# Agent attention with experts on one core: sums as a column, blocks in the last batch, first queries behind the keys

## The chip, the cores and the metric

The kernel runs on one core of a Trainium2 chip. The metric is the device time of one execution in microseconds; the median of the runs is compared.

## What is computed

Agent attention for B = 4 batches of N = 11456 tokens with D = 128 channels and 49 agents, then a mixture of 8 experts (128 to 1024 to 128) in which each token goes to one expert.

```
def sm(a, b):
    s = scale * (a @ b.transpose(0, 2, 1))
    s = s - s.max(-1, keepdims=True)
    e = np.exp(s)
    return e / (e.sum(-1, keepdims=True) + 1e-09)
a2k = sm(agents, k)
agent_v = a2k @ v
q2a = sm(q, agents)
x = q2a @ agent_v
...
expert_idx = np.argmax(x @ w_gate, axis=1)
...
h = np.maximum(xe @ w1[e], 0.0)
out[mask] = gate_w[mask, None] * (h @ w2[e])
```

`gate_w` is the softmax of the logits at the chosen expert. Inputs and output are float32.

## The kernel before

**Tiling.** A batch's tokens lie in 12 chunks, eleven of 1024 (a tile of 128 partitions with 8 tokens each) and one of 192. Keys, values and queries are loaded by SP, a chunk at a time, into one ring of 13 buffers, `ld`. A chunk of keys or queries is scaled by powers of two and split into a high and a low float16 part (ACT makes the high one, L470, DVE the low one, L475; the scalings are POOL's, L462 and L464), turned by a transposing transfer, and multiplied with the agents on PE.

**Keys and values.** DVE keeps a running maximum of the key scores (`mx`, L563); `keymax` (L568 to L582) reduces it over everything. Then for each chunk: subtraction on DVE (L590), exponential on ACT (L595), an addition of the exponentials into `es` (L602, L605: on DVE in batch 0, on POOL later), and value products on PE (`values`, L618: eight pairs of float32 products of 128 columns a chunk). `agentvalues` reduces `es`, sums it over partitions with a product by ones, and divides. `choose` then takes the expert that most tokens of the batch are likely to want; its weights are split in the same manner, and the agents' values are multiplied into its first layer (`Ah` and `Al`, L881).

**Queries.** Scores (L531 to L533), maximum and exponential (L722, L723, L728), high and low half of the weights (`ehigh`, L738; `elow`, L746), a transposing transfer into `M`.

**Dense experts.** The chosen expert is applied to all tokens of the batch, in 23 groups of up to 512 tokens by 8 slices of the hidden layer: 184 steps a batch. A step is layer 1 (two products of 512 columns, L1465 and L1466), the high half of its result on ACT (`upper`, L1472), the low half on DVE (`lower`, L1477), and five steps later layer 2 (12 products of 128 columns, L1490) into a PSUM buffer `py` of the ring `Y`, which has two. At a group's end `store` (L1499) multiplies by the factors and `put` (L1507) sends 256 KB to the output.

**Leftovers.** Tokens that chose another expert are ranked (`ranks`), gathered by POOL (L332) into blocks of 128 tokens of one expert, and computed again: for a block, two loads of weights of 512 KB (`weights_ahead`), two splits (`weights_split`: ACT L1318, DVE L1321, the latter 1.28 us), layer 1 in two halves of 12 products (L1330 to L1332), its halves on ACT (L1337) and DVE (L1341), layer 2 (L1351 to L1353) into a `pyb` of the same ring `Y`, a scaled copy (`block_store`, L1358), and a scatter by POOL (`block_out`, L1368). Twelve blocks come from the first three batches and the first part of the fourth's table, two from the last batch.

**What sets the order.** Every piece is an entry of a `Plan`: a rank in steps of the dense experts, an engine, a cost, what it needs, and which buffers it takes and frees. `Plan.order` runs a simulated clock and lets each engine, when free, take the ready piece of lowest rank; the pieces are then written into each engine's queue in that order, and an engine executes its queue in order. Pieces of DVE other than those of the steps get DX = 8 added to the rank. SP's queue holds all loads, transposes and puts together. Before, blocks' products need the last layer 1 and layer 2 of the last batch (`("L1", z0 - 1)`, `("L2", z0 - 1)`), so they stand behind all of it; the weights of the first seven blocks are fetched and some split during the last batch.

Of the kernel before, what the change touches and what calls it, by code (L numbers as in the profile page):

```python
# [31 lines left out]
SPLIT0 = (True, False)  # L32
NQ = 2
M1E, M2E, M2L, ESE = 'D', 'DP', 'D', ['D', 'P']
# [8 lines left out]
DX, AX_, WSP = 8, 0, 1  # L43

LAG = 5

LT, LTS = 140, 6
# [134 lines left out]
def agent_moe_kernel(ctx, tc, q, k, v, agents, wg, w1, w2, out):  # L182
# [174 lines left out]
    def pick(x, c):  # L357
# [6 lines left out]
                mm0=1, mm1=1, cum=1, acc=1, es=1, mx=1, m1=1, lmax=1, W=2, ag=1, pd=2, ss=4, sck=6, scq=6, fr=2)  # L364
    plan = Plan(caps, ("S", "ld", "hl", "hTk", "hTq", "M", "mm0", "mm1", "Y", "sck", "scq", "cum"))
# [1335 lines left out]
```

## Time and profile before

| | |
|---|---|
| median of 2 runs | 1139.47 us (1138.49 to 1140.44) |
| the profiled execution | 1148.7 us, span 1146.9 us |
| busy over the span | PE 1036.3 us (90%), DVE 992.8 (87%), ACT 759.0 (66%), POOL 186.1 (16%) |
| front, to the first layer 1 | 0 to 83 us |
| four batches | from 83, 331, 574 and 817 us |
| tail with the blocks | about 1075 to 1146.9 us |

All times inside the kernel are microseconds from the span's start. A busy PE is counted by modelled ends of its matmuls. The granted clock is TensorE's, as a share of full speed; a stage below 1.00 had stretches at the lower of its two levels. Chains of waits follow the work that ended last back in time; a wait names who was waited for.

### The profile page before, as it was taken

How to read it: one execution, taken by the hardware profiler on the slowest of the kernel's cores; microseconds unless marked ns; L12 is line 12 of the kernel's file. 1: busy time of each engine (PE TensorE's matmuls, PEld its weight loads, DVE VectorE, ACT ScalarE, POOL GpSimd, SP SyncE). 2: the span in 40 equal slices, each digit the busy share in tenths (PEclk: the TensorE clock that was granted, in tenths of full speed). 3: DMA queues.
4: the chain of work that ended last, by engine and by line, in shares of the span. 5: the costliest groups of instructions: out<-in, count | busy, mean ns of one | idle time of the engine just before them, and what ended most of it. 6: DMA issues, size and time to landing. Idle time of an engine off the chain costs nothing.

```text
span 1146.9 us, 34925 instructions
## 1 busy us (share of the span) xinstructions
PE 1036.3 (90%) x14260; PEld 824.1 (72%) x14260; DVE 992.8 (87%) x2213; ACT 759.0 (66%) x1350; POOL 186.1 (16%) x367
## 2 busy tenths in 40 slices
PE   7659999999989999999989999999998788999774
PEld 7537777877767778777767777777776657777774
DVE  4778999997999999969999999878998797899774
ACT  6447878666678786765877886656665456575462
POOL 1000102033101110323011010331001311100132
PEclk8779999999999999999999999999999899999887
DMA  8438979793678969763778988726564545342440
GB/s 338 132 123 185 220 197 210 179 267 103 202 167 189 233 164 201 227 208 99 203 179 192 197 188 222 208 85 164 128 117 126 118 95 135 105 148 91 144 160 11
DMA packets 265668, 190.97 MB, mean 167 GB/s; under 512 B 217513, under 2 KB 230306, under 8 KB 265504
## 3 DMA queue, kind: packets, MB, share of 16 engines
q1 hardware_dynamic: 263648, 185.39, 63.6%
q0 software_dynamic: 1568, 2.25, 0.9%
q8 instruction: 113, 1.85, 0.7%
q10 hardware_dynamic: 288, 1.05, 0.2%
q14 instruction: 51, 0.42, 0.1%
HBM read 99.75 MB, written 36.43 MB: 119 GB/s over the span
## 4 chain that ended last, share of the span: by engine, by line
PE 53%; DVE 19%; DMA 16%; issue 8%; ACT 3%; POOL 1%; SPq 0%; POOLq 0%; ACTq 0%; DVEq 0%
PE py L1490 25%; PE ph L1465 8%; PE ph L1466 8%; DMA hT<-hl 7%; DVE hh L1477 7%; DMA M<-mm 4%; PE ps_small L618 3%; DMA ld<-in_q_dram 2%; ACT hh L1472 1%; PE ps_small L531 1%; PE ps_acc L618 1%; DMA ld<-in_k_dram 1%; DVE wsp L1321 1%; DVE hl L475 1%; PE ps_small L533 1%
## 5 line engine op out<-in xcount | busy, mean ns | idle before, releaser
L1490 PEld LDWEIGHTS <-hh 128*128 128x128 f16 x8640 | 536.1, 99 | 146.8 <-issue 14.8
L1490 PE MATMUL py<-w2h,hh 128*128 128x128 f16 (+1 forms) x5760 | 595.5, 220 | 4.4 <-DVE yo L1499 1.9
L1472 ACT ACTIVATE hh<-ph 128x512 f16<-128x512 f32 (+1 forms) x736 | 412.8, 583 | 243.9 <-PE ph L1466 213.2
L1490 PE MATMUL py<-w2l,hh 128*128 128x128 f16 (+1 forms) x2880 | 520.4, 220 | 0.7 <-issue 0.7
L1477 DVE SCALAR_TENSOR_TENSOR hh<-ph,hh 128x512 f16<-128x512 f32 (+1 forms) x736 | 472.0, 668 | 50.3 <-ACT hh L1472 47.6
L1465 PE MATMUL ph<-M,Ah 128*128 128x512 f16 (+1 forms) x736 | 277.0, 377 | 30.0 <-DVE hh L1477 26.5
L1466 PE MATMUL ph<-M,Al 128*128 128x512 f16 (+1 forms) x736 | 277.2, 377 | 1.7 <-DVE Al L881 1.7
L462 POOL TENSOR_SCALAR mul<-hb 128x1 int32<-128x1 int32 (+1 forms) x90 | 27.7, 308 | 494.5 <-DVE hb L455 477.4
L475 DVE SCALAR_TENSOR_TENSOR hl<-ld,mul,hl 128x1024 f16<-128x1024 f32 (+1 forms) x84 | 102.8, 1232 | 4.7 <-ACT hl L470 4.1
L1466 PEld LDWEIGHTS <-Al 128*128 128x128 f16 x736 | 72.2, 98 | 45.8 <-issue 38.5
L436 ACT ACTIVATE jk<-ld 128x1024 f16<-128x1024 f32 (+1 forms) x90 | 90.5, 1006 | 18.6 <-DMA ld<-in_q_dram 9.3
L470 ACT ACTIVATE hl<-ld,mul 128x1024 f16<-128x1024 f32 (+1 forms) x84 | 91.0, 1093 | 12.8 <-POOL mul L462 10.8
L1465 PEld LDWEIGHTS <-Ah 128*128 128x128 f16 x736 | 72.9, 99 | 14.5 <-issue 4.0
L531 PE MATMUL ps_small<-agh,hT 128*128 128x49 f16 (+1 forms) x630 | 58.5, 186 | 13.0 <-DMA hT<-hl 12.6
L531 PEld LDWEIGHTS <-hT 128*128 128x128 f16 (+1 forms) x630 | 51.6, 98 | 22.6 <-DMA hT<-hl 19.9
L1499 DVE TENSOR_TENSOR yo<-py,cs 128x512 f32<-128x512 f32 (+1 forms) x92 | 61.6, 669 | 2.0 <-PE py L1490 2.0
L533 PE MATMUL ps_small<-agh,hT 128*128 128x49 f16 (+1 forms) x630 | 58.1, 185 | 0.0
L532 PE MATMUL ps_small<-agl,hT 128*128 128x49 f16 (+1 forms) x630 | 58.1, 185 | 0.0
L532 PEld LDWEIGHTS <-hT 128*128 128x128 f16 (+1 forms) x630 | 50.9, 98 | 2.5 <-issue 0.6
L533 PEld LDWEIGHTS <-hT 128*128 128x128 f16 (+1 forms) x630 | 50.6, 97 | 0.0
L605 POOL TENSOR_TENSOR es<-es,S 128x392 f32<-128x392 f32 (+1 forms) x33 | 35.0, 1060 | 61.7 <-ACT S L595 61.0
L728 ACT ACTIVATE E<-E,ln,div 128x392 f32<-128x392 f32 (+1 forms) x48 | 33.0, 687 | 16.6 <-DVE E L723 15.8
(293 smaller groups left out, 1262.8 us busy)
## 6 DMA issues: line engine op xcount, KB each, us to landing
ld<-in_k_dram SPq DMA_DIRECT2D x44, 512.0 KB
ld<-in_q_dram SPq DMA_DIRECT2D x44, 512.0 KB
ld<-in_v_dram SPq DMA_DIRECT2D x44, 512.0 KB
out_dram<-yo SPq DMA_DIRECT2D x88, 256.0 KB
w1e<-in_moe_w_dram SPq DMA_DIRECT2D x17, 512.0 KB
w2e<-in_moe_w_dram SPq DMA_DIRECT2D x17, 512.0 KB
exps<-E SPq DMA_DIRECT2D x44, 196.0 KB
wn<-in_moe_w_dram SPq DMA_DIRECT2D x16, 512.0 KB
```

The lines of the kernel that those rows point to most:

```text
L436: nc.scalar.activation(jk[:p, :t * D], x[:p, :t, :].rearrange("p t d -> p (t d)"), AF.Square, accum_out=ss[:p])
L470: nc.scalar.activation(hl[:p, 0, :t, :], loaded[b, src, c][:p, :t, :], AF.Copy, scale=SC[src, c][0][:p, :1])
L475: nc.vector.scalar_tensor_tensor(hl[:p, 1, :t, :], loaded[b, src, c][:p, :t, :], SC[src, c][0][:p, :1], hl[:p, 0, :t, :], op0=ALU.mult, op ...
L531: nc.tensor.matmul(o, x[:, 0, i, :p], AG["h"], start=True, stop=False)
L532: nc.tensor.matmul(o, x[:, 0, i, :p], AG["l"], start=False, stop=False)
L533: nc.tensor.matmul(o, x[:, 1, i, :p], AG["h"], start=False, stop=True)
L1465: nc.tensor.matmul(ph[:, :nn], st['Ah'][:, f, :], m, start=True, stop=False)
L1466: nc.tensor.matmul(ph[:, :nn], st['Al'][:, f, :], m, start=False, stop=True)
L1472: nc.scalar.activation(hh[:, 0, :nn], ph[:, :nn], AF.Relu)
L1477: nc.vector.scalar_tensor_tensor(hh[:, 1, :nn], ph[:, :nn], 0.0, hh[:, 0, :nn], op0=ALU.max, op1=ALU.subtract)
L1490: mm_ = lambda l, r, **k: nc.tensor.matmul(o, l, r, skip_group_check=True, **k)
L1499: nc.vector.tensor_tensor(yo[:p, :n, :], py[:p, :n * D].rearrange("p (i d) -> p i d", d=D), cs.unsqueeze(2).broadcast_to([p, n, D]), op=AL ...
```

## The change

1. **Sums as a column.** A tile of values gets a 129th column of ones (`column`, written by POOL once the load has landed), the value products have 129 columns, and so has the accumulator. The sum of the exponentials is then the accumulator's last column; it is spread over the partitions by one product. `kexp3` with `es`, and the reduction in `agentvalues(0)`, are gone. A load of values writes 512-byte runs at a pitch of 516 bytes.
2. **First queries.** All key loads come before the first query's; the first two query chunks get ranks behind the keys.
3. **Blocks.** The products of the twelve early blocks get ranks within the last batch, from step 86 on, one in eight steps; weights are loaded 22 steps ahead of them and split 10 steps ahead, into buffers of `hTk` and `ld`. The last two stay behind the batch. The last batch's ranks and table come earlier and closer together.
4. **Engines.** In batches 0 to 2 every third store of a group goes from DVE to ACT, as four operations of 128 columns; in the last batch all. There `elow` goes from DVE to POOL.
5. **Costs and landing times** of the plan are changed, and the ring `Y` no longer serves its users in the order of their ranks.

```diff
-SPLIT0 = (True, False)
+K0 = 'UWUWUWUWUWUW'
+KO = (0, 1, 2, 3, 4, 5, 6, 7, 8, 9, 10, 11)
+KLO = (0, 1, 2, 3, 4, 5, 6, 7, 8, 9, 10, 11)
 NQ = 2
-M1E, M2E, M2L, ESE = 'D', 'DP', 'D', ['D', 'P']
+M1E, M1L, M2E, M2L, SE, SEL = 'D', 'D', 'DP', 'P', 'DDA', 'A'
+K0D, Q0, QF = 0, (-332, -296), -3
...
+LANDH, LANDM, LANDL = 2.0, 2.4, 2.4
...
-LT, LTS = 140, 6
+LT, LTS, LT3, LTS3 = 140, 6, 112, 1.5
...
-FE, FG, FGI = 24, 30, 28
-FL, FW, FWJ, WA, FS, SPA = 155, 92, 10.5, 7, 14, 7
-BL = 2
+FE, FG, FGI, FGS = 24, 30, 28, 2
+FL, FLI = 124, 1
+BB, BS, BLAG, BZ, WL, WS = 86, 8, 3, 3, 22, 10
+SLOT = ('hTk', 'ld')
...
-            x = loaded[b, src, c] = ldp.tile([P, 8, D], F32, tag="ld", name="ld")
-            nc.sync.dma_start(x[:p, :t, :], chunk_view({"k": k, "v": v, "q": q}[src][b], c))
...
+            x = loaded[b, src, c] = ldp.tile([P, 8, D + (src == "v")], F32, tag="ld", name="ld")
+            nc.sync.dma_start(x[:p, :t, :D], chunk_view({"k": k, "v": v, "q": q}[src][b], c))
...
+        def column(c):
+            _, p, t = chunks[c]
+            nc.gpsimd.memset(loaded[b, "v", c][:p, :t, D:], 1.0)
...
-        def kexp3(c):
-            _, p, t = chunks[c]
-            sc = S[c][:p, :t, :]
...
-            else:
-                es = AV["es"]
-                (nc.vector if pick(ESE[b > 0], c) == "D" else nc.gpsimd).tensor_tensor(
-                    es[:p, :t, :], es[:p, :t, :], sc, op=ALU.add)
...
-                nc.tensor.matmul(ps[r:r + w, :D], sc[:p, i * A:i * A + w], x[:p, i, :],
+                nc.tensor.matmul(ps[r:r + w, :D + 1], sc[:p, i * A:i * A + w], x[:p, i, :],
...
-                nc.vector.tensor_copy(acc, ps[:64 + A, :D])
+                nc.vector.tensor_copy(acc, ps[:64 + A, :D + 1])
...
-            if i == 0:
-                e1 = one.tile([P, A], F32, tag="e1", name="e1")
-                nc.vector.tensor_reduce(e1, AV["es"].rearrange("p t a -> p a t"), axis=AX.X, op=ALU.add)
...
-                nc.tensor.matmul(AV["pe"][:, :A], ones, AV["e1"], start=True, stop=True)
+                nc.tensor.matmul(AV["pe"][:, :A], AV["acc"][:64 + A, D:].broadcast_to([64 + A, P]), both[:64 + A], start=True, stop=True)
...
-                t, u = -390 + 4 * c, chunks[c][2] / 8
-                add(n_("load", "k", c), t - 4, "SP", 0.4, load, "k", c, take=[("ld", n_("k", c))], land=2.2, move=1.3)
+                t, u = -390 + 4 * KO.index(c), chunks[c][2] / 8
+                add(n_("load", "k", c), -395 + KLO.index(c), "SP", 0.4, load, "k", c, take=[("ld", n_("k", c))], land=2.2, move=1.3)
...
+            add(n_("column", c), base + t - 1, "POOL", 0.15, column, c, r=[n_("load", "v", c)])
...
+                t = Q0[c]
             else:
...
-                    t = max(t, -7 + c)
+                    t = max(t, QF + c)
...
-            tag = slots[(2 * u + j) % len(slots)]
+            tag = SLOT[j]
...
-            nc.vector.tensor_tensor(yo[:p, :n, :], py[:p, :n * D].rearrange("p (i d) -> p i d", d=D),
-                                    cs.unsqueeze(2).broadcast_to([p, n, D]), op=ALU.mult)
+            if pick(SEL if b + 1 == B else SE, g) == "D":
+                nc.vector.tensor_tensor(yo[:p, :n, :], py[:p, :n * D].rearrange("p (i d) -> p i d", d=D),
+                                        cs.unsqueeze(2).broadcast_to([p, n, D]), op=ALU.mult)
+            else:
+                for i in range(n):
+                    nc.scalar.activation(yo[:p, i, :], py[:p, i * D:(i + 1) * D], AF.Copy, scale=cs[:, i:i + 1])
...
-            add((b, "store", g), i + LAG + 0.7, "DVE", 0.6 * u, store, g, r=[("L2", i), (b, "factors", cl)], free=[("Y", (b, g))], take=[("yo", (b, g))])
+            se = pick(SEL if b + 1 == B else SE, g)
+            add((b, "store", g), i + LAG + 0.7, "DVE" if se == "D" else "ACT", 0.6 * u if se == "D" else 0.27 * n, store, g, r=[("L2", i), (b, "factors", cl)], free=[("Y", (b, g))], take=[("yo", (b, g))])
...
-        t = b * steps + LT
+        t, ts = b * steps + (LT3 if b + 1 == B else LT), LTS3 if b + 1 == B else LTS
         for i, (g, w) in enumerate(((x, 2.6), (x, 2.9), (x, 4.4), ("PE", 0.55), ("DVE", 1.1), ("SP", 0.5), ("DVE", 0.6), ("DVE", 0.6), ("DVE", 0.5))):
-            add(("ranks", b, i), t + LTS * i, g, w, next, gen, None,
...
-        t = l0 + FG + FGI * k_ if early else l0 + FL + 3
+        t = l0 + FG + FGI * k_ if early else l0 + FL + 5 * FLI
...
-            add(p + (i, "e"), t + 2 * i, g, w, go, r=r, **kw)
...
-        t = l0 + FW + FWJ * u if u < WA else l0 + steps + 3 * u - 40
-        add(("wa", u), t, "SP", 3.0, weights_ahead, u, r=[e] + ([("wa", u - 1)] if u else []), take=[("ld", ("wb", u, 0)), ("ld", ("wb", u, 1))], land=2.2, move=2.6,
-            head=("L1", l0 + min(int(FW + FWJ * u - 4), steps - 20)))
...
+            add(p + (i, "e"), t + (FGS if early else FLI) * i, g, w, go, r=r, **kw)
...
     for u in range(NS):
...
+        late = u >= NSE
+        t = z0 + 1 + BZ * (u - NSE) if late else l0 + BB + BS * u
+        y = "1" if late else "0"
+        add(("wa", u), t - WL, "SP", 2.0, weights_ahead, u, r=["table" + y] + ([("wa", u - 1)] if u else []), take=[("ld", ("wb", u, 0)), ("ld", ("wb", u, 1))],
+            land=2.4, move=2.6, head=("L1", int(min(t - WL - 6, z0 - 20))))
...
+            x, tag = (u, j), SLOT[j]
+            add(("wu",) + x, t - WS + 2 * j, "ACT", 1.05, weights_split, u, j, True, r=[("wa", u), "bscales" + y], take=[(tag, ("wsp",) + x)])
+            add(("wl",) + x, t - WS + 2 * j + 1, "DVE", 1.2, weights_split, u, j, False, r=[("wu",) + x], free=[("ld", ("wb", u, j))])
...
-            x, t = (u, hf), z0 + 2.4 * u + 1.2 * hf
-            add(("b1",) + x, t, "PE", 0.68, block_layer1, u, hf, r=[("g", g0, 18, "e"), ("wl", u, 0), ("L1", z0 - 1)] + ([("b1", u, 0)] if hf else [("b1", u - 1, 1)] if u else []),
...
+            add(("b1",) + x, t + 1.2 * hf, "PE", 0.68, block_layer1, u, hf, r=[("g", g0, 18, "e"), ("wl", u, 0)] + ([("b1", u, 0)] if hf else [("b1", u - 1, 1)] if u else []),
+                take=[("H", ("b",) + x)], free=[(SLOT[0], ("wsp", u, 0))])
...
+            add(("b2",) + x, t + BLAG + 1.2 * hf, "PE", 0.68, block_layer2, u, hf, r=[("bd", u, 0), ("bd", u, 1), ("wl", u, 1)] + ([("b2", u, 0)] if hf else [("b2", u - 1, 1)] if u else []),
...
+        add(("bs", u), t + BLAG + 2, "DVE", 0.3, block_store, u, r=[("b2", u, 1)], free=[("Y", ("b", u))])
+        add(("bo", u), t + BLAG + 6, "POOL", 1.2, block_out, u, r=[("bs", u)] + ([(B - 1, "put", g) for g in range(NG)] if late else []), land=1.5, move=0.2)
```

The first place is DVE's queue at the front, where the key scores' last part is (`S` and `mx` of 96x98 are the last key chunk's, `mq`, `E` and `mm` belong to the first query chunk, `m` to the reduction over the keys). Before:

```order
L722 TENSOR_REDUCE mq<-ps_small 128x8
L723 TENSOR_TENSOR E<-ps_small,mq 128x392
L551 COPY S<-ps_y 96x98
L563 TENSOR_TENSOR mx<-mx,S 96x98
L738 CAST mm_143<-E 128x8x49
L746 TENSOR_TENSOR mm_143<-E,mm_143 128x8x49
L568 TENSOR_REDUCE m_769<-mx 128x49
L574 TENSOR_REDUCE m_775<-ps_small 49x1
L576 TENSOR_SCALAR dg<-ident,m_775 49x49
L582 COPY mxb<-ps_small 128x49
L590 TENSOR_TENSOR S<-S,mxb 128x392 x6
```

After:

```order
L560 COPY S<-ps_y 96x98
L572 TENSOR_TENSOR mx<-mx,S 96x98
L577 TENSOR_REDUCE m_736<-mx 128x49
L464 TENSOR_SCALAR hb<-ss 128x1
L583 TENSOR_REDUCE m_747<-ps_small 49x1
L585 TENSOR_SCALAR dg<-ident,m_747 49x49
L591 COPY mxb<-ps_small 128x49
L599 TENSOR_TENSOR S<-S,mxb 128x392 x2
L484 SCALAR_TENSOR_TENSOR hl<-ld,mul,hl 128x1024
L599 TENSOR_TENSOR S<-S,mxb 128x392 x9
L599 TENSOR_TENSOR S<-S,mxb 96x98
L716 TENSOR_REDUCE mq<-ps_small 128x8
```

The last key's copy and maximum and the reduction now stand ahead of the first query's low part (`hl`), maximum and weights; they have one scaling of the query (`hb`) between them.

The second place is DVE's queue where blocks are computed (`wsp` are split weights, `hh<-ph` with L1341 before and L1338 after is a block's low half, with L1477 before and L1474 after that of a dense step, `yb` a block's scaled copy). Before, behind the last batch:

```order
L1358 TENSOR_SCALAR yb<-pyb,fgt 128x128 x3
L1321 SCALAR_TENSOR_TENSOR wsp<-w2e,tsm_17172,wsp 128x1024
L1321 SCALAR_TENSOR_TENSOR wsp<-w1e,tsm_17157,wsp 128x1024
L1321 SCALAR_TENSOR_TENSOR wsp<-w2e,tsm_17172,wsp 128x1024
L1321 SCALAR_TENSOR_TENSOR wsp<-w1e,tsm_17157,wsp 128x1024
L1321 SCALAR_TENSOR_TENSOR wsp<-w2e,tsm_17172,wsp 128x1024
L1321 SCALAR_TENSOR_TENSOR wsp<-w1e,tsm_17157,wsp 128x1024
L1321 SCALAR_TENSOR_TENSOR wsp<-w2e,tsm_17172,wsp 128x1024
L1321 SCALAR_TENSOR_TENSOR wsp<-w1e,tsm_17157,wsp 128x1024
L1341 SCALAR_TENSOR_TENSOR hh<-ph,hh 128x512
L1321 SCALAR_TENSOR_TENSOR wsp<-w2e,tsm_17172,wsp 128x1024
L1341 SCALAR_TENSOR_TENSOR hh<-ph,hh 128x512 x5
```

After, within the last batch:

```order
L1474 SCALAR_TENSOR_TENSOR hh<-ph,hh 128x512
L1318 SCALAR_TENSOR_TENSOR wsp<-w1e,tsm_17223,wsp 128x1024
L732 CAST mm_144<-E 96x2x49
L1474 SCALAR_TENSOR_TENSOR hh<-ph,hh 128x512 x2
L1318 SCALAR_TENSOR_TENSOR wsp<-w2e,tsm_17247,wsp 128x1024
L1338 SCALAR_TENSOR_TENSOR hh<-ph,hh 128x512
L1474 SCALAR_TENSOR_TENSOR hh<-ph,hh 128x512
L1338 SCALAR_TENSOR_TENSOR hh<-ph,hh 128x512
L1474 SCALAR_TENSOR_TENSOR hh<-ph,hh 128x512 x3
L1355 TENSOR_SCALAR yb<-pyb,fgt 128x128
L1318 SCALAR_TENSOR_TENSOR wsp<-w1e,tsm_17223,wsp 128x1024
L1474 SCALAR_TENSOR_TENSOR hh<-ph,hh 128x512
```

Splits that stood in a row now stand between dense steps' low halves; `mm` is a query chunk's high half.

The third place is POOL's queue at the front (L462/L464 before and L471/L473 after are the scalings of keys and queries; MEMSET of `ld` writes the column of ones). Before:

```order
L462 TENSOR_SCALAR mul<-hb 128x1
L464 TENSOR_SCALAR div<-hb,bits 128x1
L462 TENSOR_SCALAR mul<-hb 128x1
L464 TENSOR_SCALAR div<-hb,bits 128x1
L462 TENSOR_SCALAR mul<-hb 128x1
L464 TENSOR_SCALAR div<-hb,bits 128x1
L602 COPY es<-S 128x392
L462 TENSOR_SCALAR mul<-hb 128x1
L464 TENSOR_SCALAR div<-hb,bits 128x1
L462 TENSOR_SCALAR mul<-hb 128x1
```

After:

```order
L473 TENSOR_SCALAR div<-hb,bits 128x1
L471 TENSOR_SCALAR mul<-hb 128x1
L473 TENSOR_SCALAR div<-hb,bits 128x1
L394 MEMSET ld 128x8 x6
L471 TENSOR_SCALAR mul<-hb 128x1
L473 TENSOR_SCALAR div<-hb,bits 128x1
L394 MEMSET ld 128x8 x4
L394 MEMSET ld 96x2
L471 TENSOR_SCALAR mul<-hb 128x1
L473 TENSOR_SCALAR div<-hb,bits 128x1
```

The first addition into `es` is gone, and writes of the column, each of which needs its chunk of values landed, stand ahead of the later scalings.

## Rows read from the trace of the kernel before

**Rows 1.** Windows by stage: us, busy (instructions) of PE, PEld, DVE, ACT, POOL, clock, DMA share, GB/s

```profile
83.00:331.00 248.00, 237.37 (x3391) 185.82 (x3391) 225.41 (x466) 183.62 (x324) 43.45 (x91) 0.98 0.79 192
331.00:574.00 243.00, 235.57 (x3367) 184.60 (x3367) 221.82 (x481) 177.85 (x317) 42.85 (x91) 1.00 0.78 190
574.00:817.00 243.00, 232.97 (x3318) 182.27 (x3318) 219.14 (x468) 173.58 (x305) 41.09 (x89) 1.00 0.72 174
817.00:1075.00 258.00, 230.65 (x2940) 178.14 (x2940) 227.26 (x559) 150.12 (x282) 32.47 (x46) 0.96 0.47 120
1075.00:1147.00 72.00, 46.20 (x683) 44.93 (x681) 45.68 (x82) 34.33 (x52) 18.68 (x16) 0.82 0.32 101
```

**Rows 2.** Waits of the last batch (817 to 1074): waiting, waited for, us, times, longest

```profile
PE ph L1465 <- DVE hh L1477: 18.9, 14, 3.1
...
DVE mq L722 <- PE py L1490: 5.4, 1, 5.4
...
DVE fr L1231 <- DMA fg<-ranks,fri: 4.0, 1, 4.0
```

**Rows 3.** The same view of the second batch (331 to 574)

```profile
PE ph L1465 <- DVE hh L1477: 3.2, 3, 1.6
```

**Rows 4.** A window of the tail, columns as in the first group

```profile
1095.00:1105.00 10.00, 4.66 (x74) 4.26 (x72) 10.00 (x10) 9.71 (x12) 4.12 (x2) 0.81 0.57 174
```

**Rows 5.** Windows of the splits on line 1321 alone, in the tail

```profile
1075.00:1147.00 72.00, 19.55 (x16) 0.82 0.32 101
```

**Rows 6.** Timeline of DVE at the front: start, us, engine, line, operation

```profile
40.41 0.27 DVE L425 SCALAR_TENSOR_TENSOR agl<-ps_small,mul,agh 128x49 f16<-128x49 f32 x1
44.69 0.57 DVE L722 TENSOR_REDUCE mq<-ps_small 128x8 f32<-128x392 f32 x1 [4.00 <-PE ps_small L533]
...
46.05 0.26 DVE L563 TENSOR_TENSOR mx<-mx,S 96x98 f32<-96x98 f32 x1
...
47.58 0.81 DVE L568 TENSOR_REDUCE m<-mx 128x49 f32<-128x392 f32 x1
```

**Rows 7.** Chain of waits from 36 to 90 us: start, us, what

```profile
51.82 12.43 PE ps_acc L618 x179
...
69.24 6.67 DMA w2e<-in_moe_w_dram
...
81.36 2.47 DVE hl L475 x2
83.83 1.33 DVE Al L881 x2
```

**Rows 8.** Timeline of the end, all engines

```profile
1135.93 0.22 PE L1353 MATMUL pyb<-wsp,hh 128*128 128x128 f16 x1
```

**Rows 9.** Lines of the last batch, DVE: xcount, busy us, mean ns, idle before

```profile
L1499 DVE TENSOR_TENSOR yo<-py,cs 128x512 f32<-128x512 f32 (+1 forms) x25 | 16.8, 670 | 0.0
...
L746 DVE TENSOR_TENSOR mm<-E,mm 128x392 f16<-128x392 f32 (+1 forms) x11 | 5.9, 536 | 0.1
```

**Rows 10.** Chain of waits in the last batch

```profile
821.63 2.40 DVE hh L1477 x4
...
1047.06 1.34 PE py L1490 x24
```

**Rows 11.** Lines of the tail: the nearest ACT operations of 128 columns

```profile
L1297 ACT ACTIVATE xs<-fxT,mul 128x128 f16<-128x128 f32 x2 | 0.7, 394 | 1.6 <-DVE mul L324 1.6
L1284 ACT ACTIVATE jk<-fxT 128x128 f16<-128x128 f32 x2 | 0.6, 310 | 0.1
```

**Rows 12.** Windows with DMA full: loads of 4 KB runs, then a write of 724-byte runs

```profile
4.00:16.00 12.00, 8.79 (x64) 8.12 (x63) 4.85 (x17) 8.05 (x15) 0.91 (x4) 0.85 1.01 404
1057.00:1058.00 1.00, 1.00 (x16) 0.77 (x14) 1.00 (x3) 0.60 (x1) 0.00 (x0) 1.00 1.05 298
```

**Rows 13.** SP's waits from 940 to 1075 us

```profile
SPq L1507 <- DVE yo L1499: 52.9, 9, 12.8
```

**Rows 14.** Lines of the second batch: the value products

```profile
L618 PE MATMUL ps_small<-ld,S 128*64 128x128 f32 (+2 forms) x180 | 12.4, 279 | 0.0
```

More of the change, by code (lines that the diff above doesn't have):

```diff
@@ L646, in agentvalues @@
                 AV["pv"] = small_ps()
-                nc.tensor.matmul(AV["pv"][:, :A], AV["acc"][:64 + A], both[:64 + A], start=True, stop=True)
+                nc.tensor.matmul(AV["pv"][:, :A], AV["acc"][:64 + A, :D], both[:64 + A], start=True, stop=True)
             elif i == 4:
@@ L911, in chain @@
             add(n_("lower", *x), base + t + d[3], "DVE", 1.15 * u + 0.1, lower, *x, r=[n_("upper", *x)], free=[("ld", n_(*x))])
-            add(n_("turn", *x), base + t + d[4], "SP", 2.9 if u == 1 else 2.4, turn_over, *x, r=[n_("lower", *x)], take=[("hT" + src, n_(*x))],
-                free=[("hl", n_(*x))], land=1.3, move=3.0 if u == 1 else 0.8)
+            add(n_("turn", *x), base + t + d[4], "SP", 3.05 if u == 1 else 2.5, turn_over, *x, r=[n_("lower", *x)], take=[("hT" + src, n_(*x))],
+                free=[("hl", n_(*x))], land=LANDH, move=3.0 if u == 1 else 0.8)
+        order = KO if first else tuple(range(NCK))
         def key_chunk(c, t, kcost):
@@ L981, in attention @@
             add(n_("kexp2", c), base + t + 0.3, "ACT", 0.52, kexp2, c, r=[n_("kexp", c)])
-            g = "D" if c == 0 and False else pick(ESE[b > 0], c)
-            g = "POOL" if c == 0 or g != "D" else "DVE"
-            add(n_("kexp3", c), base + t + 0.7, g, 0.5 if g == "DVE" else 1.15, kexp3, c, r=[n_("kexp2", c), n_("kexp3", c - 1) if c else None],
-                take=[("es", n_())] if c == 0 else [], free=[("S", n_("k", c))])
-            add(n_("values", c), base + t + 0.6, "PE", 0.88 * u + 0.1, values, c, r=[n_("kexp2", c), n_("load", "v", c)],
+            add(n_("column", c), base + t - 1, "POOL", 0.15, column, c, r=[n_("load", "v", c)])
+            add(n_("values", c), base + t + 0.6, "PE", 0.88 * u + 0.1, values, c, r=[n_("kexp2", c), n_("load", "v", c), n_("column", c)],
                 take=([("Y", n_("acc"))] if c == 0 else []) if first else [("s", n_("v", c))], free=[("S", n_("k", c)), ("ld", n_("v", c))])
@@ L1049, in attention @@
                     (qexp, 7, "ACT", 0.62, None, dict(free=[("scq", n_("q", c))])),
-                    (ehigh, 8, "DVE", 0.28, None, dict(take=[(m_, n_("q", c))])),
+                    (ehigh, 8, "DVE" if pick(M1L if last else M1E, c) == "D" else "ACT", 0.28 if pick(M1L if last else M1E, c) == "D" else 0.45, None, dict(take=[(m_, n_("q", c))])),
                     (elow, 9, "POOL" if pick(M2L if last else M2E, c) == "P" else "DVE", 1.0 if pick(M2L if last else M2E, c) == "P" else 0.5,
                      None, dict(free=[("S", n_("q", c))])),
-                    (eturn, 10, "SP", 1.25, None, dict(take=[("M", n_("q", c))], free=[(m_, n_("q", c))], land=1.3, move=1.5))):
+                    (eturn, 10, "SP", 1.3, None, dict(take=[("M", n_("q", c))], free=[(m_, n_("q", c))], land=LANDM, move=1.5))):
                 add(n_(f.__name__, c), base + t + d[e], g, w, f, c, r=r or [prev], **kw)
@@ L1639, in agent_moe_kernel @@
-        add(("bs", u), t + 2.4 * BL + 1, "DVE", 0.3, block_store, u, r=[("b2", u, 1)], free=[("Y", ("b", u))])
-        add(("bo", u), t + 2.4 * BL + 2, "POOL", 1.2, block_out, u, r=[("bs", u)], land=1.5, move=0.2)
+        late = u >= NSE
[3 more added lines that the diff above has]
+            land=2.4, move=2.6, head=("L1", int(min(t - WL - 6, z0 - 20))))
```

72 lines of the change are left out of this document (32 added, 40 removed).

## The prediction, made before the changed kernel ran

> **What bounds the kernel now.** I read the busy times by stage first, then the waits, then the chain of waits. The stages are the four batches (from 83, 331, 574 and 817 us) and a tail in which the leftover blocks are computed [rows 1]. In the second and third batch PE is busy for 236 and 233 of 243 us and DVE for 222 and 219 (0.91 and 0.90); both are full, the granted clock is 1.00, and little that leaves either engine alone shows in the time. The last batch is another thing: it has no next keys and values to prepare, yet takes 258 us. PE is busy for 231 of them (0.89), and the waits say why: layer 1 waits 18.9 us for a PSUM buffer that DVE's residual (L1477) frees late [rows 2], against 3.2 us in the second batch [rows 3]. DVE was not overloaded but held: by a first reduction over queries, 5.4 us, and by the gathered table, 4.0 us, both with residuals queued behind them.
>
> The tail is 72 us with PE at 46 busy, DVE at 46 and a clock of 0.82; with two levels, 1.2 and 2.4 GHz, that is about a third of the tail at the lower one. A stretch of ten microseconds in it shows DVE full, ACT at 9.7 and PE at 4.7 [rows 4]: the two split the weights of the next blocks, 16 splits or 19.6 us of DVE in the tail [rows 5], while PE has nothing to multiply, and then PE multiplies while DVE has little. So the tail costs 72 us for work of which no engine needs more than 46.
>
> At the front, DVE stands still for 4.00 us until the first query chunk's scores come, and the last key's copy and maximum and the reduction over all keys (L568) stand behind it [rows 6]. The first value products start at 51.82 us, 12.43 us of them follow on PE, then the weights' load, then two residuals of queries (L475, 2.47 us) ahead of the two operations that make Al (L881), without which layer 1 cannot start [rows 7].
>
> **The change part by part.**
>
> *Twelve blocks within the last batch.* Nothing of their work goes away; it moves under the batch's own. The sum is therefore made over the last batch and tail together. They run from 817 to the last product, which ends at 1136.15 [rows 8]: 319 us. DVE has 227.3 + 45.7 = 273.0 us of work in them. Two edits take some away: 23 stores move to ACT, 23 x 0.60 us = 13.7 (busy time 0.67 [rows 9], but neighbours overlap: four residuals of that size start 0.60 apart, 2.40 in all [rows 10]), and the 11 lower halves of the queries' weights move to POOL, 5.9 us [rows 9], some 5 without the overlap. That leaves 254 us. PE has 230.7 plus 14 blocks of 48 products; 24 such take 1.34 us at the full clock [rows 10], so 2.7 us a block and 37.5 in all: 268.
>
> If both engines reach the shares of the second and third batch, DVE needs 254 / 0.905 = 281 us and PE 268 / 0.97 = 276. I take 279, and 319 - 279 = **40 us gained**. What would fall short: the shares of today's last batch, DVE 0.88, PE 0.89, give 289 and 301, so a gain of 18 to 30. What would exceed it: DVE at 0.95, 267 us, a gain of 52. I choose the middle since the work then comes spread, one block in eight steps, as the order shows, and DVE's splits lie between residuals instead of eight in a row. The last two blocks still come at the end, and the 10.75 us from 1136.15 to the span's end (an output copy, a scatter, the end of the program) stay.
>
> *Stores on ACT.* Four operations of 128 columns replace one of DVE's. The nearest rows take 0.31 and 0.40 us each [rows 11], so 1.2 to 1.6 us against 0.67. In the last batch ACT has 150 + 34 us [rows 1] and gets some 33 more in 279: 0.78, under what DVE carries. In the earlier batches a third of the stores moves, 7 of 23: DVE saves 4.7 us a batch, ACT gains 10 on 178. PE, at 0.97, takes most of that saving as idle DVE. I put +0.8 us a batch, **2.5 us** in all; the ends are -5 (a store that leaves late holds one of the two y buffers, and the next group's layer 2 waits) and +12 (DVE was the bound after all).
>
> That y ring is the new wait within the last batch too: blocks now take y buffers between groups, so a group's layer 2 can begin only when the store of the group before it has left ACT, 1.2 to 1.6 us and whatever ACT has in front of it. The block's own second layer (1.34 us) covers most of it. I leave 0 to 1.5 us x 12, inside the ends above. The Trainium skill ("Trainium Kernel Development and Optimization", Best Practices) warns that regular bubbles can mean that PSUM has run out; no run here shows it for this ring yet.
>
> *Sums as a 129th column.* For batches 1 to 3 it removes POOL work alone, which nothing waited for: nothing gained. In batch 0 it removes eleven DVE additions, in the shadow of the PE-bound value products (12.43 us [rows 7]), and the reduction of those sums. It adds the sum by a product after the accumulator's copy, some 0.4 us in a row at the front. It also changes v's loads, from 4 KB runs to 512-byte runs at a pitch of 516. The nearest rows: loads in 4 KB runs move 404 GB/s with the DMA engines full; a write in runs of 724 bytes moves 298 [rows 12]. A chunk of 524 KB so goes from 1.30 to 1.76 us, 5 us a batch at a DMA share of 0.72 to 0.79: hidden, taken at nothing; its other end is in the rivals.
>
> The Trainium skill ("DMA: Bandwidth & Descriptors", How a descriptor splits into AXI transactions) says that a piece that starts off a 256-byte boundary drags unused bytes along: 512 bytes become three transactions and up to 24 beats in place of 16. If it applied to the written side, an estimate by that page is 1.95 us a chunk, 7 us a batch. No trace here shows it.
>
> *First queries behind the keys.* The 4.00 us wait goes from in front of the key maximum, and with it the query's own reduction and weights [rows 6]. Without them DVE is free at 40.7 (the row before the wait), copies and takes the last maximum in 0.5 us and reduces at 41.3 in place of 47.58: **6.3 us**. Al no longer stands behind two residuals: 2.2. Less 0.4 for the sum's product. What can come back: the first query's own chain ends later, and chunk 1's weights M with it, up to 3 us; and POOL's column writes, which wait for v's landings (the last near 40 us by the rates above), stand ahead of the query's scalings. Taken: **6.5**; ends 2 and 9.
>
> *Costs and landing times in the plan, 'Y' not strict:* these only choose order; their effect is in the order above.
>
> **Sum.** 40 + 6.5 + 2.5 = 49 us. The profiled execution took 1148.7 us (span 1146.9), 9 above the median of 1139.5; its span would become 1098. I take the same gain from the median: 1139.5 - 49 = 1090.5, rounded to **1090**. The low ends together (18 + 2 - 5 = 15) give 1124, the high ones (52 + 9 + 12 = 73) 1067.
>
> **Rivals.**
> 1. *The last batch as disturbed as today.* DVE's order still holds gathers and the queries' reductions; a block's residual waits behind them too, and the y ring adds. The 18.9 us of layer 1's waits [rows 2] speak for it; that DVE loses its stores there speaks against. A gain of 24 (the middle of 18 to 30) + 6.5 = 30.5: 1109. Chance 0.22.
> 2. *The odd width costs.* If f32 products of 129 columns took twice as long, the value products' 12.4 us a batch [rows 14] would double: +12 at the front, where they are on the path, and up to +12 in each of three batches where PE is full, 48 in all: 1138, no gain left. If only v's last chunk lands late at the front, some 5 us: 1095, inside my range. Nothing in the trace shows a width of 129. Chance 0.05 for the doubling.
> 3. *The other side: blocks' weights late.* SP issues in order, and a y put that waits for its store holds whatever follows: 52.9 us in 9 waits, the longest 12.8, in the last batch today [rows 13]. A block's weights are ranked 12 steps ahead of their first split. A step of the last batch takes 279 / 184 = 1.5 us, so 18 us, less 6.67 for landing (the start-up's, the one the chain shows [rows 7]), leaves 11. A later load stops ACT and DVE, which go in order, and every group behind. The 49 us are gone when 12 blocks lose 4.1 us each, so when SP holds a load for 15 us on average; that is the point from which the kernel is slower. At 17 us they lose 6 each: 1090 + 72 = 1162. Only the longest of today's waits is near. Chance 0.03.
> 4. *Better than that.* DVE at 0.95 and the front in full: 52 + 9 + 2.5 = 63.5: 1076. Chance 0.15.
>
> **Numbers.** My forecast (1080 to 1100) has 0.50, the rivals 0.22, 0.05, 0.03 and 0.15; the 0.05 left lie between rival 1 and no gain. The range 1072 to 1113 takes in the forecast, rival 4's middle and most of rival 1; about 0.07 lie below it and 0.13 above. A difference of under 2% (23 us) counts as no change: faster means below 1116.7. That is the forecast, rival 4 and nearly all of rival 1 with a part of the rest: 0.88. Same 0.09, slower 0.03.
>
> **What would show it.** Right: from the last batch's first layer 1 to the last product some 280 us, clock near 1.00 in it, hardly a tail; DVE near 0.9 busy there; no run of eight wsp splits; first value product near 45.5; POOL without es. Wrong: PE's layer 1 or 2 waiting for y stores on ACT or for wsp; SP waits in front of w1e loads; waits of value products for v or for the column; the batches from 83 to 817 longer than 734 us; L618's products above 280 ns each.

## The result and the profile after

The changed kernel takes **1093.28 us** (median of 1090.36 and 1096.21) against 1139.47 before: a ratio of 0.9595, interval 0.9479 to 0.9711, so 46 us less. The forecast was 1090. Four more runs on another chip gave 0.9607 (0.9569 to 0.9644). The total is as predicted; two of its terms are not, and by luck they offset each other.

The profiled execution took 1090.4 us, span 1088.7. Windows by stage, columns as in [rows 1]; the fourth line is the last batch with its tail, the fifth the first three batches together:

```profile
77.00:315.00 238.00, 234.94 (x3383) 185.62 (x3383) 218.78 (x464) 190.43 (x354) 31.52 (x91) 0.99 0.82 198
315.00:554.00 239.00, 234.24 (x3369) 185.00 (x3368) 216.03 (x471) 183.92 (x344) 29.84 (x91) 1.00 0.81 194
554.00:791.00 237.00, 233.44 (x3342) 184.70 (x3341) 212.74 (x461) 178.93 (x332) 29.20 (x90) 0.99 0.78 182
791.00:1078.00 287.00, 262.88 (x3612) 215.25 (x3609) 254.62 (x600) 206.22 (x426) 63.21 (x71) 0.99 0.48 130
77.00:791.00 714.00, 702.62 (x10087) 555.31 (x10088) 647.54 (x1394) 553.27 (x1029) 90.56 (x272) 0.99 0.81 191
```

The tail is gone: the last product starts at 1077.4, 7.8 us behind the last layer 1, and the end of 11 us is as before. But from 77 to 791 the three earlier batches also became shorter, by 20 us, which was not forecast.

The first profile of the kernel before lay 9 us above its median, so a second was taken (e9_before, 1138.25 us, span 1136.6). The two kernels, two profiles each, by the first layer 1 of each batch and the last product:

| us | before, first | before, second | after, first | after, second (e0_after) |
|---|---|---|---|---|
| front, to the first layer 1 | 82.9 | 82.2 | 77.1 | 79.4 |
| three batches | 734.5 | 732.6 | 714.3 | 716.4 |
| last batch and tail | 318.5 | 311.0 | 286.0 | 287.8 |
| end | 11.0 | 10.8 | 11.3 | 11.3 |
| span | 1146.9 | 1136.6 | 1088.7 | 1094.9 |

The first profile's excess was nearly all in the last batch and tail (318.5 against 311.0), the stage on which the largest term was worked out. Between the second profiles, the front gives 3 us, the three batches 16, the last batch and tail 23.

### The profile page after: what moved, and what is told of

Same layout as the page of the kernel before. It is cut to its first block, busy times and chain, and to the rows that moved or that the text cites. A ratio compares the mean times of both kernels' runs of the same rounds, so it can differ in the third digit from the quotient of the medians.

```text
span 1088.7 us, 35016 instructions
## 1 busy us (share of the span) xinstructions
PE 1014.8 (93%) x14260; PEld 814.4 (75%) x14260; DVE 948.0 (87%) x2142; ACT 797.8 (73%) x1524; POOL 162.5 (15%) x390
## 5 line engine op out<-in xcount | busy, mean ns | idle before, releaser
L1474 DVE SCALAR_TENSOR_TENSOR hh<-ph,hh 128x512 f16<-128x512 f32 (+1 forms) x736 | 472.4, 668 | 50.3 <-ACT hh L1469 47.9
L471 POOL TENSOR_SCALAR mul<-hb 128x1 int32<-128x1 int32 (+1 forms) x90 | 25.3, 281 | 514.3 <-DVE hb L464 471.1
L740 POOL TENSOR_TENSOR mm<-E,mm 128x392 f16<-128x392 f32 (+1 forms) x30 | 26.2, 872 | 219.7 <-DVE mm L732 101.1
L540 PE MATMUL ps_small<-agh,hT 128*128 128x49 f16 (+1 forms) x630 | 57.1, 184 | 1.1 <-ACT hh L1469 0.8
L542 PE MATMUL ps_small<-agh,hT 128*128 128x49 f16 (+1 forms) x630 | 56.9, 184 | 0.0
L540 PEld LDWEIGHTS <-hT 128*128 128x128 f16 (+1 forms) x630 | 51.1, 97 | 5.7 <-DMA hT<-hl 2.6
L1501 ACT ACTIVATE yo<-py,cs 128x128 f32<-128x128 f32 x174 | 49.7, 375 | 3.2 <-PE py L1487 1.8
L541 PEld LDWEIGHTS <-hT 128*128 128x128 f16 (+1 forms) x630 | 49.8, 97 | 2.5
L542 PEld LDWEIGHTS <-hT 128*128 128x128 f16 (+1 forms) x630 | 49.6, 96 | 0.0
```

The source lines that it names most:

```text
L540: nc.tensor.matmul(o, x[:, 0, i, :p], AG["h"], start=True, stop=False)
L541: nc.tensor.matmul(o, x[:, 0, i, :p], AG["l"], start=False, stop=False)
L542: nc.tensor.matmul(o, x[:, 1, i, :p], AG["h"], start=False, stop=True)
L1474: nc.vector.scalar_tensor_tensor(hh[:, 1, :nn], ph[:, :nn], 0.0, hh[:, 0, :nn], op0=ALU.max, op1=ALU.subtract)
L1501: nc.scalar.activation(yo[:p, i, :], py[:p, i * D:(i + 1) * D], AF.Copy, scale=cs[:, i:i + 1])
```

## The experiments

Each kernel was timed in turn with the kernel before on the same chip. Chips differ (before took 1138.6, 1139.6 and 1147.4 us on the three used), so the ratio to before is what can be compared; 0.001 is 1.1 us, and intervals are 0.002 to 0.005 to each side.

**e0_after.** The changed kernel once more.

> The changed kernel again, as the base on this chip. If its two first times (1090 and 1096 us) show its spread, it lies at 1090 to 1097 us.

1096.1 us, ratio 0.9607. As expected; it is the base for the others.

**e9_before.** The kernel before once more, one profile.

> The kernel before once more, for a second profile of it. Its first profile lay 9 us above the median. If that was a slower front (82.9 us to the first layer 1, where the kernel with only the blocks moved shows 78.5 with the same front), the front is near 78.5 here and the batches stay at 243 to 249 us; if it was the tail, that is shorter.

1138.25 us. The excess of the first profile was in the tail's stage, not in the front (82.2 again), so the second condition held.

### The last batch: moving the blocks, or relieving DVE?

**e1_blocks_behind.** The changed kernel, blocks as before behind the last batch:

```diff
-            add(("b1",) + x, t + 1.2 * hf, "PE", 0.68, block_layer1, u, hf, r=[("g", g0, 18, "e"), ("wl", u, 0)] + ...
+            add(("b1",) + x, t, "PE", 0.68, block_layer1, u, hf, r=[("g", g0, 18, "e"), ("wl", u, 0), ("L1", z0 - 1)] + ...
...
-        t = z0 + 1 + BZ * (u - NSE) if late else l0 + BB + BS * u
+        t = l0 + FW + FWJ * u if u < WA else l0 + steps + 3 * u - 40
```

> The changed kernel with the blocks' products, splits and weight loads back behind the last batch, all else as changed. Theory (the blocks' move gives what the last batch gained, 32 us in the two profiles, and DVE's relief alone gives little since the tail stays): 1118 to 1128 us. Rival (it is the relief of DVE in the last batch by stores on ACT and low halves on POOL that gave most of it, the move only little): 1098 to 1108 us.

1108.5 us, ratio 0.973: 14 us more than the changed kernel by the ratios (12 by the medians), at the rival's upper end. The last batch takes 243.3 us and the tail 56.0.

**e8_only_blocks.** The kernel before with the blocks' ranks of the changed one, the reverse of the edit above; DVE keeps stores and low halves.

> The kernel before with the blocks alone moved into the last batch (ranks and table earlier, the y ring served as in the changed kernel); stores and low halves stay on DVE. Theory (DVE sets the last batch: 273 us of work at a share of 0.905 are 302 us in place of 319): a gain of 10 to 20, 1120 to 1130 us. Rival (the blocks fill gaps whatever DVE has to do): a gain of 28 to 34, 1106 to 1112 us.

1142.55 us, ratio 1.0031 (1.0009 to 1.0054). Neither: moving the blocks alone gives nothing, a hair is lost. The last batch and tail take 315.7 us, between the two profiles of before (311.0 and 318.5). This run also has the earlier table and the ring `Y` served as in the changed kernel, so the three together give nothing.

**e5_last_stores_dve.** The changed kernel with the last batch's stores on DVE.

```diff
-M1E, M1L, M2E, M2L, SE, SEL = 'D', 'D', 'DP', 'P', 'DDA', 'A'
+M1E, M1L, M2E, M2L, SE, SEL = 'D', 'D', 'DP', 'P', 'DDA', 'D'
```

> The changed kernel with the last batch's stores back on DVE, blocks still within the batch. Theory (DVE's work sets the last batch): 13.7 us at a share of 0.9 are 15 us, 1108 to 1114 us. Rival (the stores only need to leave DVE when its queue has blocks between; PE is the bound at 0.91): 1096 to 1102 us.

1111.65 us, ratio 0.976: 17 us more for 13.7 us of DVE's work, by the theory 15. The theory holds, with somewhat more than its price.

**e6_last_elow_dve.** The same line with `M2L = 'D'`.

> The changed kernel with the last batch's low halves of queries' weights back on DVE. Theory (DVE's work sets the last batch, as 13.7 us of stores cost 15.6): 5 to 6 us of work, 1100 to 1104 us. Rival (POOL's slower form delays the weights' transfer as much as DVE gains): 1093 to 1098 us.

1107.27 us on the slowest chip, ratio 0.9635 (0.9586 to 0.9683): 3 us more by the ratios, with intervals that overlap. Its last batch and tail took 300.4 us; those of e3_queries_first, which has the changed kernel's code in that stage and ran on the same chip, 293.8. It points the theory's way, but does not settle it.

DVE's load shows what these have in common. Windows of DVE and the others over the last batch and tail, columns as in [rows 1], of e9_before, e1_blocks_behind, e8_only_blocks, e5_last_stores_dve and e0_after in turn:

```profile
815.00:1126.00 311.00, 272.75 (x3620) 221.57 (x3618) 271.53 (x637) 184.67 (x334) 49.33 (x61) 0.95 0.45 123
```

```profile
796.00:1095.00 299.00, 268.29 (x3601) 219.24 (x3599) 254.80 (x597) 206.22 (x424) 57.76 (x69) 0.96 0.46 125
```

```profile
816.00:1132.00 316.00, 275.19 (x3620) 223.13 (x3618) 273.32 (x638) 185.53 (x334) 52.14 (x61) 0.95 0.44 121
```

```profile
794.00:1101.00 307.00, 269.92 (x3603) 220.16 (x3600) 267.25 (x620) 185.31 (x335) 59.61 (x70) 0.96 0.45 122
```

```profile
796.00:1084.00 288.00, 267.21 (x3602) 218.97 (x3600) 254.02 (x598) 205.69 (x424) 62.55 (x70) 0.96 0.47 130
```

DVE's share is 0.873, 0.852, 0.865, 0.870 and 0.882. Over all fourteen profiles it is 0.85 to 0.89, so the stage takes DVE's work divided by such a share. That is not the whole account: 254 us of work give 285 to 299 us by it, and where in this range the stage lies depends on the place of the blocks (299 behind the batch, 288 within, at the same work). Behind the batch, the dense steps take 243.3 us, near the pace of the other batches (237 to 240), and the tail 56.0; within it, the batch is stretched by 37 us and the tail shortened by 48. The relief, some 18 us of DVE's work, is worth 12 us with the blocks behind the batch (311 to 299) and 28 with the blocks within (316 to 288), both with what else of the change acts there, such as the costs; e5_last_stores_dve, which differs from the changed kernel in the stores alone, shows 19 (307 to 288). The move is worth 11 to 14 us once DVE is relieved, and nothing when it is not.

What kept the share under 0.905 shows in the waits of DVE in the last batch and tail, first of e0_after, then of e8_only_blocks (waiting, waited for, us, times, longest):

```profile
DVE hh L1474 <- ACT hh L1469: 12.6, 18, 2.2
DVE fr L1228 <- DMA fg<-ranks,fri: 4.3, 2, 2.4
DVE hh L1338 <- ACT hh L1334: 3.0, 6, 0.9
```

```profile
DVE fr L1234 <- DMA fg<-ranks,fri: 14.0, 4, 4.5
DVE hh L1480 <- ACT hh L1475: 10.5, 21, 1.5
```

The longest row, the waits for ACT's high halves, is not what sets this stage apart: the second batch of e0_after (318 to 558 us), which has no blocks, has as much of it.

```profile
DVE hh L1474 <- ACT hh L1469: 14.1, 32, 1.3
```

What the earlier batches do not have are the waits for gathered rows, 4.3 us, and those of the blocks' own low halves, 3.0. Together they are the 7 us by which 288 exceeds 254 / 0.905; that they cause it is argued from the waits, no run took them out. The waits for gathered rows, with the dense steps' low halves queued behind, are 4.3 us in e0_after and 14.0 in e8_only_blocks; over all profiles they go from 3 to 14. PE then waits for those low halves, 12.3 us in e0_after (before 18.9 [rows 2]) and 23.3 in e8_only_blocks:

```profile
PE ph L1462 <- DVE hh L1474: 12.3, 12, 2.2
```

```profile
PE ph L1468 <- DVE hh L1480: 23.3, 12, 4.1
```

### The three batches before: stores, or the plan's costs?

**e4_stores_dve.** The changed kernel with `SE = 'D'`: batches 0 to 2 store on DVE again.

> The changed kernel with the stores of batches 0 to 2 back on DVE (the last batch's stay on ACT). Theory (DVE bounds the earlier batches: 4.7 us of stores at a share of 0.905 are 5.2 us a batch, most of the 20 us that the three batches gained between the two profiles): those batches 243 us each again, 1110 to 1116 us. Rival (the gain comes from the plan's costs and landing times): no change, 1092 to 1098 us. The prediction's own term (PE is the bound there, 0.8 us a batch): 1097 to 1100 us.

1099.91 us, ratio 0.9653 (0.9611 to 0.9694): 5 us more by the ratios, within both intervals' reach of none. The three batches take 718.7 us, 2 to 4 more than in the changed kernel's profiles. That fits the prediction's own term, and it is not the 20.

**e7_costs_before.** The changed kernel with the costs and landing times of before:

```diff
-LANDH, LANDM, LANDL = 2.0, 2.4, 2.4
+LANDH, LANDM, LANDL = 1.3, 1.3, 2.2
```

(and 0.33 for 0.7 of the scalings, 2.9 for 3.05 of the transposes' issue, 1.25 for 1.3.)

> The changed kernel with the plan's costs and landing times of before (transposes 1.3 us to land, loads 2.2, scalings 0.33). Theory of the stores: no change, 1092 to 1098 us. Theory of the costs: most of the 20 us of the three batches comes back, 1108 to 1116 us.

1110.96 us, ratio 0.9742 (0.9702 to 0.9783): 15 us more, and the three batches take 734.4 us again, while the front (78.0) and the last batch with its tail (287.4) stay as in the changed kernel. The theory of the costs holds.

**e10_only_landing.** The kernel before with two numbers changed:

```diff
-                free=[("hl", n_(*x))], land=1.3, move=3.0 if u == 1 else 0.8)
+                free=[("hl", n_(*x))], land=2.0, move=3.0 if u == 1 else 0.8)
...
-                    (eturn, 10, "SP", 1.25, None, dict(take=[("M", n_("q", c))], free=[(m_, n_("q", c))], land=1.3, move=1.5))):
+                    (eturn, 10, "SP", 1.25, None, dict(take=[("M", n_("q", c))], free=[(m_, n_("q", c))], land=2.4, move=1.5))):
```

> The kernel before with two numbers of the plan changed alone: a turned chunk of keys or queries is taken to land 2.0 us after its transfer instead of 1.3, the queries' weights 2.4 instead of 1.3. Theory (PE stood in its queue waiting for transposing transfers, 12.4 us in the first three batches of the second profile of before and 3.5 in the changed kernel; put later in the order, they are landed when PE comes to them): PE's waits for them fall below 5 us, 1125 to 1131 us. Rival (it is the other costs, the scalings' 0.7 and the loads' 2.4, that gave the 15 us): 1135 to 1142 us.

1139.08 us where before took 1147.44: ratio 0.9932 (0.9904 to 0.996), 8 us less. That is the theory's direction, at the low end of its size, and half of the 15 us. The three batches take 723.3 us, 9 less than in e9_before. PE's waits for transposing transfers in them, of e9_before, e7_costs_before, e10_only_landing and the changed kernel's two profiles in turn:

```profile
PE ps_small L758 <- DMA M<-mm: 7.5, 8, 1.5
PE ps_small L531 <- DMA hT<-hl: 4.9, 8, 1.1
```

```profile
PE ps_small L752 <- DMA M<-mm: 9.1, 9, 3.8
...
PE ps_small L540 <- DMA hT<-hl: 3.5, 6, 1.5
```

```profile
PE ps_small L531 <- DMA hT<-hl: 3.9, 8, 0.9
...
PE ps_small L758 <- DMA M<-mm: 1.4, 2, 1.2
```

```profile
PE ps_small L752 <- DMA M<-mm: 1.7, 3, 1.3
...
PE ps_small L540 <- DMA hT<-hl: 0.2, 1, 0.2
```

```profile
PE ps_small L540 <- DMA hT<-hl: 2.6, 5, 0.9
...
PE ps_small L752 <- DMA M<-mm: 0.9, 1, 0.9
```

12.4 and 12.6 us with the old numbers, 5.3 with the two new ones alone, 1.9 and 3.5 with all. In the plan's simulated clock a transpose is landed after the number given; with 1.3 PE's queue has the product at a place where the transfer is not yet there, and everything behind it stands. With a later landing the plan puts other steps in front. The other half of the 15 us, from the remaining numbers or from their working together with the rest of the change, was not separated.

### The column and the first queries

**e2_es_kept.** The changed kernel with `kexp3`, `es`, `agentvalues(0)`, loads in 4 KB runs and 128 columns, as before (no column, no 129th value).

> The changed kernel with the exponentials' sums kept in es (DVE in batch 0, POOL later), values loaded in 4 KB runs and products of 128 columns. Theory (hidden on both sides but for the front): within 3 us of the changed kernel. Rival (the column takes POOL's and DVE's work off the path): 5 to 12 us more. Rival (512-byte runs cost time in the batches): 3 to 8 us less.

1091.79 us, ratio 0.9591 against 0.9607: no difference that can be told. The price of the loads is there all the same. Windows at the front in which values are loaded, of the changed kernel:

```profile
20.00:32.00 12.00, 11.91 (x163) 11.57 (x163) 9.79 (x21) 9.60 (x20) 1.72 (x16) 1.00 1.18 290
```

290 GB/s against 404 for 4 KB runs [rows 12]; 524 KB take 1.81 us. In the three batches it is hidden (715.2 us in e2_es_kept, 714.3 and 716.4 with the column). At the front it is not. The first query is loaded behind the values, and DVE's one scaling `hb` of it stands in front of the rest of the reduction over the keys. On one chip, e6_last_elow_dve (with the column) and e11_es_kept_ehigh_act (without it; the two differ otherwise in the last batch's engines alone) show the loads of values from 24 to 28 us (columns as in [rows 1]) and then `hb` in DVE's timeline:

```profile
24.00:28.00 4.00, 4.00 (x73) 3.92 (x74) 3.60 (x7) 2.36 (x6) 0.00 (x0) 1.00 1.22 292
41.88 0.15 DVE L464 TENSOR_SCALAR hb<-ss 128x1 int32<-128x1 int32 x1 [5.99 <-ACT jk L445]
```

```profile
24.00:28.00 4.00, 4.00 (x55) 3.94 (x55) 3.41 (x6) 2.78 (x7) 0.00 (x0) 1.00 1.02 419
37.08 0.15 DVE L461 TENSOR_SCALAR hb<-ss 128x1 int32<-128x1 int32 x1
```

The first value product starts at 44.8 us with the column and at 40.3 without, the first layer 1 at 78.8 and 75.3. So the column costs some 3 us of the front there; in the whole time this is not clear of the noise.

The odd width costs nothing: the value products by line, of the kernel before and of the changed one (ns, min/median/max):

```profile
L618 PE MATMUL ps_small<-ld,S x540: 272/273/323, 242.7 to 774.4; 128*64 128x128 f32 x89, 128*49 128x128 f32 x88, 96*49 96x128 f32 x3
```

```profile
L616 PE MATMUL ps_small<-ld,S x540: 271/273/324, 226.5 to 747.3; 128*64 128x129 f32 x89, 128*49 128x129 f32 x88, 96*49 96x129 f32 x3
```

**e3_queries_first.** The changed kernel with ranks and first loads of the queries as before:

```diff
-K0D, Q0, QF = 0, (-332, -296), -3
+K0D, Q0, QF = 0, (-345, -298), -7
...
-                add(n_("load", "k", c), -395 + KLO.index(c), "SP", 0.4, load, "k", c, take=[("ld", n_("k", c))], land=2.2, move=1.3)
+                add(n_("load", "k", c), t - 4, "SP", 0.4, load, "k", c, take=[("ld", n_("k", c))], land=2.2, move=1.3)
```

> The changed kernel with the first queries' ranks and the order of the first loads as before. The prediction's term (6.5 us at the front, 2 to 9): first layer 1 at 82 to 86 us in place of 77 to 79, 1098 to 1105 us. Rival (the front's end is set by the choice of the expert and the weights' load, not by the query): within 2 us of 1096.

1110.57 us, ratio 0.9682 (0.9632 to 0.9732): 8 us more, and the first layer 1 at 84.7 us where e0_after, on another chip, has 79.4; DVE waits 4.03 us for the first query's scores again. But fronts differ by how the first products run (last section: 16 of them take 3.63 us in some profiles, about 2 in others), and the term has to be read at like starts. The first layer 1, in us, over all profiles:

| first 16 products | order of before | new order, with the column | new order, without it |
|---|---|---|---|
| 3.63 us | 82.9, 82.2; e3_queries_first 84.7 | 79.4, 77.3 | |
| 1.97 to 2.57 us | 78.5 (e8_only_blocks), 78.4 (e10_only_landing) | 77.1, 78.0, 78.8, 78.8, 79.7 | 77.2, 75.3 |

With the 3.63 us the new order gains 3 to 7 us, and the rival (nothing) falls. With the faster start the order of before, without the column, is as quick as the new one with it, and the rival holds; without the column on both sides the new order gains 1 to 3. In e6_last_elow_dve the reduction over the keys starts at 35.1 us, 7 earlier than the 42.2 of e10_only_landing, and then waits 6 for the late query. The rest of the 8 us by which the ratios differ does not lie in the front and is not explained.

**e11_es_kept_ehigh_act.** e2_es_kept with `M1L = 'A'`, the last batch's high halves on ACT.

> The changed kernel with es kept (1091.8 us by itself), and in the last batch the high halves of the queries' weights on ACT in place of DVE. Theory (DVE's work sets the last batch): 11 or 12 copies of 0.35 us at a share of 0.9 are 4 us less, 1086 to 1090 us. Rival (ACT is by now as much in the way, its residuals' first halves come later): 1091 to 1097 us.

1098.55 us on the slowest chip, ratio 0.9571 (0.9527 to 0.9615), 2 us under e2_es_kept and 4 under the changed kernel, all within the intervals. Its last batch and tail took 295.4 us, no less than the 293.8 of e3_queries_first beside it. Its first layer 1 came at 75.3 us, 3.5 before that of e6_last_elow_dve on the same chip. Whether taking still more from DVE helps stays open; no version was shown to beat the changed kernel.

## Why the prediction was right, point by point

**The total** is right by luck, through two errors of opposite sign: 17 us too much for the blocks between the second profiles, 15 too little for the costs.

**Twelve blocks, 40 us: 23 measured between the second profiles, 32 between the first.** The sum of DVE's work was right (254 us forecast, 254.0 and 254.6 measured), and so was PE's (268; 267.2 and 262.9). The step that failed is the share: 0.905 was taken from batches without gathers, 0.88 came. That was the first rival's value, a gain of 18 to 30. The other part of the miss is the profile: the 319 us from which the gain was counted was 7.5 us long against the second one. And by the prediction's sum the move alone, with DVE's 273 us at 0.905, would have gained 17 us; e8_only_blocks shows that it gains nothing without the relief of some 18 us of DVE.

**Costs and landing times, nothing: 15 us.** The step that failed is "these only choose order; their effect is in the order above". The order was looked at where blocks and queries move, and not where PE meets a transposing transfer. Had the waits for `M` and `hT` in the batches from 83 to 817 been read, the 12 to 14 us that PE stood there were to be seen before the run.

**Stores on ACT, 2.5 us: 2 to 5.** Right within what can be told. The four operations take 376 ns each, 1.5 us for a store, inside the 1.2 to 1.6 worked out. The y ring's new wait in the last batch came to 2.9 + 0.8 us, of a bound of 18. By lines of waits of the changed kernel, the last batch and tail:

```profile
PE pyb L1348 <- ACT yo L1501: 2.9, 3, 2.1
...
PE py L1487 <- DVE yb L1355: 0.8, 2, 0.5
```

The Trainium skill ("Trainium Kernel Development and Optimization", Best Practices) warns that consistent bubbles can mean that PSUM ran out. These waits for a PSUM buffer agree with it, but they are few and small: 3.7 us of 287.

**First queries, 6.5 us: 3 to 7 when the first products take 3.63 us, nothing when they take about 2 (1 to 3 without the column).** The row from which the term was worked out came from a profile of the first kind. The mechanism came as told and one step more. Timeline of DVE in e0_after:

```profile
39.50 0.82 DVE L577 TENSOR_REDUCE m<-mx 128x49 f32<-128x392 f32 x1
42.64 0.15 DVE L464 TENSOR_SCALAR hb<-ss 128x1 int32<-128x1 int32 x1 [2.32 <-ACT jk L445]
42.71 0.27 DVE L583 TENSOR_REDUCE m<-ps_small 49x1 f32<-49x128 f32 x1
```

The reduction runs at 39.5, 8 us earlier than in [rows 6], but the query's one scaling `hb` stands between its two halves and waits 2.32 us for the squares of a query that is now loaded late, behind the values. The order showed that row; its wait was not priced. The first value product, forecast near 45.5, started at 45.1 and 45.6.

**The column, nothing: nothing that can be told in the whole time, some 3 us at the front.** The load's price was put at 1.76 us from the row with 724-byte runs and came to 1.81. The step that failed is "hidden": it was read from the batches, and at the front the first query stands behind eleven such loads. The estimate by the Trainium skill ("DMA: Bandwidth & Descriptors", How a descriptor splits into AXI transactions) was up to 1.95, 8% above what was measured.

**Rival 2** (129 columns at half rate) fell: 273 ns at either width. **Rival 3** (weights late) fell: SP did hold back, its puts waited 80.9 us for their stores in 14 waits in the last batch, the longest 14.0, yet no split waited for a load of weights. The average wait, 80.9 / 14 = 5.8 us, is under the slack of 11 and far from the 15 named. SP's waits in the last batch of the changed kernel:

```profile
SPq L1508 <- ACT yo L1501: 80.9, 14, 14.0
```

## What to carry to other kernels

Before crediting a move of work into a busy stage, divide the stage's work on its fullest engine by the share that this very stage has reached, gathers and all: here 254 us are 291 to 297 by the 0.85 to 0.87 of this stage before and 281 by the 0.905 of the other batches, and 286 to 288 came, between the two. The move paid only together with the work that left the engine, and then 11 to 14 us. Numbers that only set an order are edits like any other: look for the waits that the old order leaves on in-order queues (here PE on transposing transfers) and price what would remove them. A dearer load is hidden only where nothing waits for what is loaded behind it. And take the length of a stage from two profiles before counting a gain from it.

## What the runs showed of the hardware

The front's first products have two speeds. The same 16 float32 products of 49 columns (`ps_y`) near 14 us take 3.63 us in both profiles of before and in e0_after and 2.14 in the changed kernel's first profile, and 1.88 or 1.90 a few us later in every one of them. The timelines of PE in e9_before and in the first profile of after:

```profile
13.76 3.63 PE L529 MATMUL ps_y<-agf,xT 128*128 128x49 f32 x16
...
21.41 1.88 PE L529 MATMUL ps_y<-agf,xT 128*128 128x49 f32 x16
```

```profile
14.03 2.14 PE L538 MATMUL ps_y<-agf,xT 128*128 128x49 f32 x16
...
18.89 1.88 PE L538 MATMUL ps_y<-agf,xT 128*128 128x49 f32 x16
```

3.63 / 1.88 is 1.9, near the ratio of the two clock levels. In the first profile of before the granted clock was indeed at the lower one, 0.50, while in e9_before, with the same 3.63 us, it reads 1.00:

```profile
14.00:16.00 2.00, 2.00 (x11) 2.00 (x10) 0.66 (x2) 2.00 (x5) 0.00 (x0) 0.50 1.03 422
```

```profile
14.00:16.00 2.00, 2.00 (x11) 2.00 (x11) 0.60 (x2) 2.00 (x4) 0.00 (x0) 1.00 1.04 426
```

Why the reading differs is not shown, nor why some executions start at either speed. In the order of before the start carries through: DVE comes to the first query's wait at 39.7 us after the 3.63 (e9_before) and at 35.3 after 1.97 (e10_only_landing, with the same DVE queue up to there), and the first layer 1 came at 82.2 and 78.4. So some 4 us of that front are luck, about as much as the term that was to be measured there. In the new order, where DVE waits for the late query in either case, no such difference shows (77.3 and 79.4 against 77.1 to 79.7).
